# Neighbourhood attention beside a spatial gating unit: logits reduced by column-tiled mask matmuls, tokens strided by four, and two sets of transposes moved from TensorE to DMA

## The chip, the cores and the metric

The kernel runs on one core of one Trainium2 chip. The metric is the device time of one execution in microseconds (us). Times are quoted as medians over several executions, with the lowest and highest in brackets. A profile is one execution taken with the hardware profiler. In it PE is TensorE, PEld its weight loads, DVE is VectorE, ACT is ScalarE, POOL is GpSimd and SP is SyncE, which here only issues DMAs; SPq and ACTq are the DMA queues that SP and ACT issue to. L701 is line 701 of that run's kernel.py. PSUM (`ps`) is where this kernel's matmuls put their results; to copy out of it is called evacuation. The granted clock is the recorded share of TensorE's full clock. An execution counts as slow when it takes over 1.5% more than the fastest of the same kernel; all runs that are compared below are fast unless it is said otherwise.

## The reference

One input `x` of 2048 tokens by 512 goes through two branches, and `x` is added at the end. The inputs are bf16.

```python
def _A_ref(x, wqkv, wo):                    # attention over 8 earlier tokens, 2 apart
    H = 32; Dh = D // H; W, dil = (8, 2)
    qkv = (x @ wqkv).reshape(B, S, 3, H, Dh)...      # cut
    idx = pos[:, None] - off[None, :]; mask = idx >= 0
    logits = einsum('bhsd,bhswd->bhsw', q, kg) * scale
    logits = where(mask, logits, -1000000000.0)
    attn = softmax(logits)
    o = einsum('bhsw,bhswd->bhsd', attn, vg)
    return o.reshape(B, S, D) @ wo

def _B_ref(x, w_in, w_sp, b_sp, w_out):     # Fh = 896
    z = gelu(x @ w_in); z1 = z[..., :Fh]; z2 = layernorm(z[..., Fh:])
    g = einsum('ts,bsf->btf', w_sp, z2) + b_sp       # mixes all 2048 tokens
    return (z1 * g) @ w_out

xn = layernorm(x)
return x + _A_ref(xn, wqkv, wo) + _B_ref(xn, w_in, w_sp, b_sp, w_out)
```

There are 32 heads of 16 elements. Each token looks at 8 keys, so a logit is the sum of 16 products, and there are 2048 x 8 x 32 of them.

## The kernel before

The program hands each instruction to a small static scheduler, which fixes the order on each engine from estimated durations. Two stages follow from the data. Stage 1 makes the normalised `x`, transposes it (`xnT`), and computes Q, K, V, both gate halves (`z1`, `z2`) and the logits. Stage 2 mixes tokens with `w_sp` and multiplies out, since mixing needs all of `z2`. VectorE's attention products with V run beside stage 2.

The logits: VectorE multiplies Q with eight shifted copies of K (one operation of 128 x 4096 for each quarter of the channels). TensorE sums 16 channels to one head by taking a 128-token slice of the products as stationary weights, and an 8-column mask as the moving operand.

```python
for blk in range(4):
    for w in range(8):
        last = t.matmul(ps[:, 3072 + blk * 256 + w * 32 + 8 * c: 3072 + blk * 256 + w * 32 + 8 * c + 8],
                        AC(off["pb"] + 4096 * s_ + 512 * w + 128 * blk, [[1, 128]]), E8,
                        start=True, stop=True)
```

That is a weight load of 128 x 128 and a matmul of 8 columns, 512 times. Normalised `x` and the attention output are transposed by TensorE against an identity and copied out of PSUM by ScalarE; V is copied out by VectorE and written to a DRAM scratch, from which the eight shifted copies are loaded for each block of 128 tokens:

```python
T("dve", lambda v: v.tensor_copy(A("Vn", 512, 512 * sl).rearrange("p (d h) -> p d h", d=16),
                                 bank(k).rearrange("p (h d) -> p d h", d=16)), ...)      # V out of PSUM
...
src = bass.AP(tensor=vscr.tensor, offset=vscr.offset + (16 + 128 * b) * 512,
              ap=[[512, 128], [-1024, 8], [1, 512]])
dma("sp", lambda e: e.dma_start(A("Vs", 4096, 4096 * sv).rearrange("p (w n) -> p w n", w=8), src), ...)
...
for cc in range(4):                                       # attention output, transposed by TensorE
    last = t.matmul(ps[:, 512 * k + 128 * cc: 512 * k + 128 * cc + 128],
                    A("On", 128, 512 * so + 128 * cc), ident, start=True, stop=True)
```

`w_sp` is already transposed by DMA on its way in, four pieces of 2 MB, and the program orders transposing DMAs against all others.

## Time and profile before

The time is 260.27 us (259.58 to 260.78, three runs).

| of the profile before (span 257.5 us) | value |
|---|---|
| TensorE busy | 248.4 us, 96% |
| VectorE busy | 207.6 us, 81% |
| ScalarE busy | 98.1 us, 38% |
| stage 1 on TensorE | from 7.5 to 114.8 us |
| stage 2 on TensorE | to 253.9 us |
| moved by DMA | 39.21 MB |

The prediction shows the main lines. The groups of the kernel before, split by shape, show the logits reduction that the change takes away. The columns are line, engine, operation, destination and source, shapes and count; then busy us and mean ns of one; then idle time of the engine ahead of them.

```profile
L658 PE MATMUL ps<-arena 128*128 128x8 bf16 x512 | 15.1, 166 | 0.8 <-DVE arena L651 0.8
L658 PEld LDWEIGHTS ps<-arena 128*128 128x128 bf16 x512 | 14.9, 96 | 4.3 <-DVE arena L651 1.7
```

The 166 ns is a matmul's length from start to end; what it costs in a pipeline is the distance between starts, 25 ns here, so read costs from the timeline. The weight load of 96 ns is as dense as any other in this kernel. The V copy that moves to ScalarE is 16 x 686 ns on VectorE in the same view.

### The profile page before, as it was taken

The page shows a single profiled execution, that of the slowest core. Times are in us where ns is not written, and L with a number is a line of the kernel's source. Part 1 is how long each engine was busy: PE and PEld are TensorE (multiplying, and loading weights), DVE is VectorE, ACT ScalarE, POOL GpSimd, SP SyncE. Part 2 cuts the span into 40 slices and gives each one's busy share as a digit, 9 for nine tenths or more (in the row PEclk, how much of TensorE's full clock was granted, in tenths as well). Part 3 has the DMA queues.
Part 4 walks back from the last instruction along what each step waited for, and adds up shares of the span by engine and source line. Part 5 has one row for each costly group of instructions (what it writes and reads, how often), then busy time and mean ns, then how long its engine had stood idle before and what let it go on. Part 6 is the DMA issues. An engine that isn't in the chain of part 4 may idle for free.

```text
span 257.5 us, 4109 instructions
## 1 busy us (share of the span) xinstructions
PE 248.4 (96%) x1679; PEld 123.5 (48%) x1706; DVE 207.6 (81%) x297; ACT 98.1 (38%) x185; POOL 31.1 (12%) x57
## 2 busy tenths in 40 slices
PE   6999999999999999999999999999999999999993
PEld 1445546456654645444444444444444444444441
DVE  4859999999979989106999999996589599898651
ACT  2894369688999977773001000010000100001000
POOL 6414563310250040000000000000000000000000
PEclk9999999999999999999999999999999999999999
DMA  7991210100013989979655544789915647330321
GB/s 224 364 347 47 83 45 0 64 20 3 23 61 73 228 197 160 253 159 355 215 186 183 178 168 129 185 202 317 349 48 160 224 124 259 96 114 18 108 83 41
DMA packets 62020, 39.21 MB, mean 152 GB/s; under 512 B 34337, under 2 KB 61361, under 8 KB 62001
## 3 DMA queue, kind: packets, MB, share of 16 engines
q1 hardware_dynamic: 59568, 35.33, 48.6%
q0 software_dynamic: 800, 2.11, 2.3%
q10 hardware_dynamic: 1632, 1.51, 1.8%
q8 instruction: 13, 0.21, 0.3%
q14 instruction: 7, 0.05, 0.1%
HBM read 26.35 MB, written 4.21 MB: 119 GB/s over the span
## 4 chain that ended last, share of the span: by engine, by line
PE 85%; issue 6%; DVE 4%; POOL 1%; POOLq 1%; DMA 1%; ACT 0%; DVEq 0%
PE ps L834 37%; PE ps L890 9%; PE ps L628 8%; PE ps L706 7%; PE ps L753 6%; PE ps L894 5%; PE ps L604 5%; PE ps L658 3%; PE ps L874 1%; PE ps L589 1%; POOLq L375 1%; POOL fpool L739 1%; DVE fpool L572 1%; DMA arena<-in_A_x_dram 1%; DVE arena L651 1%
## 5 line engine op out<-in xcount | busy, mean ns | idle before, releaser
L834 PE MATMUL ps<-arena 128*128 128x512 bf16 x440 | 97.7, 379 | 0.4
L834 PEld LDWEIGHTS ps<-arena 128*128 128x128 bf16 x448 | 43.6, 98 | 51.2
L879 ACT ACTIVATE arena<-ps 128x512 bf16<-128x512 f32 x16 | 9.3, 596 | 124.2 <-PE ps L874 124.2
L858 DVE TENSOR_TENSOR arena<-arena 128x4096 bf16<-128x4096 bf16 x16 | 36.5, 2284 | 0.0
L651 DVE TENSOR_TENSOR arena<-arena 128x4096 bf16<-128x4096 bf16 x16 | 36.0, 2284 | 0.6 <-ACT arena L636 0.6
L628 PE MATMUL ps<-arena 128*128 128x512 bf16 x124 | 28.2, 379 | 0.2
L890 PE MATMUL ps<-arena 128*128 128x512 bf16 x108 | 26.4, 379 | 0.9 <-ACT arena L879 0.7
L706 PE MATMUL ps<-arena 128*128 128x448 bf16 x128 | 27.1, 352 | 0.0
L753 PE MATMUL ps<-arena 128*128 128x512 bf16 x107 | 24.4, 379 | 0.3
L841 DVE TENSOR_TENSOR arena<-ps,arena 128x512 bf16<-128x512 f32 x28 | 19.4, 692 | 4.9 <-PE ps L834 4.0
L901 DVE TENSOR_TENSOR arena<-ps,arena 128x512 bf16<-128x512 f32 x16 | 10.9, 687 | 14.7 <-PE ps L894 13.6
L636 ACT ACTIVATE arena<-ps 128x1024 bf16<-128x1024 f32 x16 | 16.3, 1020 | 10.7 <-PE ps L628 10.5
L860 DVE TENSOR_TENSOR arena<-arena 128x2048 bf16<-128x2048 bf16 x16 | 19.5, 1219 | 0.1
L628 PEld LDWEIGHTS ps<-arena 128*128 128x128 bf16 x128 | 12.4, 98 | 14.5
L758 ACT ACTIVATE arena<-ps 128x512 bf16<-128x512 f32 x28 | 16.2, 597 | 7.1 <-PE ps L753 7.1
L713 ACT ACTIVATE arena<-ps 128x448 bf16<-128x448 f32 x32 | 17.3, 543 | 1.8 <-PE ps L706 1.1
L658 PEld LDWEIGHTS ps<-arena 128*128 128x128 bf16 x512 | 14.9, 96 | 4.3 <-DVE arena L651 1.7
L890 PEld LDWEIGHTS ps<-arena 128*128 128x128 bf16 x112 | 10.6, 98 | 12.4 <-ACT arena L879 0.9
L706 PEld LDWEIGHTS ps<-arena 128*128 128x128 bf16 x128 | 11.7, 97 | 10.1 <-ACT arena L713 1.0
L753 PEld LDWEIGHTS ps<-arena 128*128 128x128 bf16 x112 | 10.6, 97 | 12.3
L894 PE MATMUL ps<-arena 128*128 128x512 bf16 x63 | 16.2, 379 | 0.1
L658 PE MATMUL ps<-arena 128*128 128x8 bf16 x512 | 15.1, 166 | 0.8 <-DVE arena L651 0.8
(59 smaller groups left out, 226.7 us busy)
## 6 DMA issues: line engine op xcount, KB each, us to landing
arena<-vscr SPq DMA_DIRECT2D x16, 1024.0 KB, 5.2
arena<-in_A_x_dram SPq DMA_DIRECT2D x28, 128.0 KB, 3.9
vscr<-arena POOLq DMA_DIRECT2D x16, 128.0 KB, 2.0
out_dram<-arena SPq DMA_DIRECT2D x16, 128.0 KB, 1.7
arena<-in_A_wqkv_dram SPq DMA_DIRECT2D x2, 512.0 KB, 10.0
arena<-in_B_w_in_dram SPq DMA_DIRECT2D x1, 896.0 KB, 11.7
arena<-in_B_w_out_dram SPq DMA_DIRECT2D x1, 896.0 KB, 11.7
arena<-in_A_x_dram ACTq DMA_DIRECT2D x4, 128.0 KB, 4.9
```

Of the source, the lines that this page charges most:

```text
L628: last = t.matmul(bank(k + which), AC(off["wqk"] + 1024 * dc + col0, [[1, 128]]), AC(off["xnT"] + dc * S + 512 * j, [[1, 512]]), start=(dc ...
L651: T("dve", lambda v: v.tensor_tensor(pbv, qb, kb, ALU.mult), reads=rd, writes=[("pb", s_)], est=c_dve(4096, 2.0), name="prod%d_%d" % (j, c ...
L658: last = t.matmul(ps[:, 3072 + blk * 256 + w * 32 + 8 * c: 3072 + blk * 256 + w * 32 + 8 * c + 8], AC(off["pb"] + 4096 * s_ + 512 * w + 12 ...
L706: last = t.matmul(ps[:, 2048 + 512 * hf: 2048 + 512 * hf + 448], AC(off["xnT"] + dc * S + 128 * b, [[1, 128]]), AC(off["w_in"] + 1792 * dc ...
L713: T("act", (lambda c0, hf: lambda a: a.activation(A("z2", 448, FH * b + c0), ps[:, 2048 + 512 * hf: 2048 + 512 * hf + 448], ACTF.Gelu_appr ...
L753: lastm = t.matmul(bank(k), AC(off["w_in"] + 1792 * dc + 128 * fc, [[1, 128]]), AC(off["xnT"] + dc * S + 512 * j, [[1, 512]]), start=(dc = ...
L834: last = t.matmul(bank(k), AC(off["z2"] + FH * sh + 128 * fc, [[1, 128]]), AC(off["wT"] + WSL * r_ + sh * 512, [[1, 512]]), start=(sh == 0 ...
L841: T("dve", lambda v: v.tensor_tensor(tgv, bank(k), A("bbc", 512, 512 * tc), ALU.add), reads=[("ps", k), "bbc"], writes=[("tg", ts_)], est= ...
L858: T("dve", lambda v: v.tensor_tensor(tv, tv, av, ALU.mult), reads=[("attn", j)], writes=[("Vs", sv)], est=c_dve(4096, 2.0), name="pv%d" % ...
L860: T("dve", lambda v: v.tensor_tensor(A("Vs", 2048, 4096 * sv), A("Vs", 2048, 4096 * sv), A("Vs", 2048, 4096 * sv + 2048), ALU.add), writes ...
L890: t.matmul(bank(k), AC(off["z1T"] + fc * S + 128 * tb, [[1, 128]]), AC(off["w_out"] + 512 * fc, [[1, 512]]), start=(fc == 0), stop=False)
L894: last = t.matmul(bank(k), AC(off["OT"] + cc * S + 128 * tb, [[1, 128]]), AC(off["wo"] + 512 * cc, [[1, 512]]), start=False, stop=(cc == 3))
```

## The change

The intent is to shorten TensorE's work. The logits get a layout with heads on partitions: the mask (128 x 32) is stationary and the products stream by, 512 columns at a time, into 32 output partitions; four token groups use four column groups of the array at once (a column group is 32 of its 128 columns, chosen here by the output partitions). Tokens of a block are now every fourth token of 512, so that a 32x32 block transpose on VectorE brings the attention weights back to tokens on partitions. The eight shifted V rows of two blocks of one parity then overlap, so one load of nine rows serves both. The diff, cut to its core:

```diff
+    def tok(b):
+        return (512 * (b // 4) + b % 4, 4) if TMAP else (128 * b, 1)
...
+            if b >= XDMA:                                  # blocks 8 to 15 of x
+                dma("sp", lambda e: e.dma_start_transpose(AC(off["xnT"] + 128 * b, [[S, 4], [1, 128]]),
+                                                          A("xn", 512, 512 * sl)), ...)
+                return
...
-                T("dve", lambda v: v.tensor_copy(A("Vn", 512, 512 * sl)...
+            T("act", lambda a: a.activation(A("Vn", 512, 512 * sl)...
...
+                    for wh in range(2):
+                        for cc in range(4):
+                            sc = (s_ - 3 + cc) % NPB
+                            for g in range(4):
+                                last = t.matmul(
+                                    PC(32 * g * PR + 3072 + 512 * wh, [[1, 512]], 32),
+                                    AC(off["E8"] + 32 * cc, [[1, 32]]),
+                                    AC(off["pb"] + 4096 * sc + 2048 * wh + 128 * g, [[512, 4], [1, 128]]),
+                                    start=(cc == 0), stop=(cc == 3))
...
+                T("dve", lambda v: v.transpose(AC(off["attn"] + 1024 * j, [[32, 8], [256, 4], [1, 32]]),
+                                               AC(off["D"] + d0, [[128, 8], [1, 4], [4, 32]])), ...)
...
+                    src = bass.AP(tensor=vscr.tensor, offset=vscr.offset + (512 * j + 2 + par) * 512,
+                                  ap=[[4 * 512, 128], [1024, 9], [1, 512]])
+                    dma("act", lambda e: e.dma_start(AC(off["Ve"] + 4608 * par, [[512, 9], [1, 512]]), src), ...)
...
-            T("pe", tr, reads=[("On", so), "ident"], ...)            # and its ScalarE copy
+            dma("sp", lambda e: e.dma_start_transpose(AC(off["OT"] + 512 * b, [[128, 4], [1, 128]]),
+                                                      A("On", 512, 512 * so)), ...)
...
-        NWARM = cfg.get("n_warm", 5)
+        NWARM = cfg.get("n_warm", 4)
```

With it come other estimates for the scheduler, other buffers (two places for `w_sp` in place of three), softmax exponentials taken two blocks at a time, x and output traffic on ScalarE's queue, the `wqk` loads ahead of the fifth to eighth block of `x`, and no ordering of transposing DMAs against plain ones.

## The prediction

> **What bounds the kernel now.** I read the busy totals of the page first, then the chain that ended last, then TensorE's timeline, and last the groups and the windows of the other engines.
>
> ```profile
> PE 248.4 (96%) x1679; PEld 123.5 (48%) x1706; DVE 207.6 (81%) x297; ACT 98.1 (38%) x185; POOL 31.1 (12%) x57
> PE 85%; issue 6%; DVE 4%; POOL 1%; POOLq 1%; DMA 1%; ACT 0%; DVEq 0%
> ```
>
> TensorE is busy 96% of 257.5 us and carries 85% of the chain. A busy PE need not be a PE at its peak, so the timeline must tell what one matmul really costs from start to start, and whether there are gaps.
>
> ```profile
> 6.30 0.40 PE L589 MATMUL ps<-arena 128*128 128x128 bf16 x4
> ...
> 37.62 1.68 PE L706 MATMUL ps<-arena 128*128 128x448 bf16 x8
> 39.13 0.61 PE L589 MATMUL ps<-arena 128*128 128x128 bf16 x8
> ...
> 57.33 0.94 PE L658 MATMUL ps<-arena 128*128 128x8 bf16 x32
> 58.13 1.67 PE L706 MATMUL ps<-arena 128*128 128x448 bf16 x8
> ...
> 114.81 24.34 PE L834 MATMUL ps<-arena 128*128 128x512 bf16 x110
> ...
> 146.33 0.39 PE L874 MATMUL ps<-arena 128*128 128x128 bf16 x4
> 146.56 7.07 PE L834 MATMUL ps<-arena 128*128 128x512 bf16 x32
> 153.46 0.39 PE L874 MATMUL ps<-arena 128*128 128x128 bf16 x4
> ...
> 251.54 1.69 PE L890 MATMUL ps<-arena 128*128 128x512 bf16 x7 [0.69 <-ACT arena L879]
> 253.06 1.03 PE L894 MATMUL ps<-arena 128*128 128x512 bf16 x4
> ```
>
> Each row is a start, a length, a line and a count. Start differences give the steps: 32 matmuls of 512 columns from 146.56 to 153.46, so 0.2157 us each; 8 of 448 columns from 37.62 to 39.13, 0.189; a group of four 128-column transposes from 146.33 to 146.56, 0.23; a group of 32 logit reductions (8 columns each) from 57.33 to 58.13, 0.80, so 0.025 each. Hardly a row shows an idle time. The kernel is thus two stretches of dense TensorE work: stage 1 (normalisation, Q, K, V, both gate halves, logits) from 7.5 to 114.8 us, stage 2 (spatial mixing and output) to 253.9, then 3.6 us of last addition and store.
>
> The engine next in line is VectorE:
>
> ```profile
> 20.00:40.00 20.00, 19.87 (x168) 10.81 (x169) 19.18 (x44) 9.97 (x17) 11.60 (x17) 1.00 0.16 55
> 40.00:60.00 20.00, 19.87 (x228) 11.55 (x229) 19.03 (x29) 16.85 (x32) 3.81 (x6) 1.00 0.08 28
> 60.00:80.00 20.00, 19.79 (x212) 11.51 (x213) 18.24 (x26) 19.01 (x40) 4.74 (x5) 1.00 0.08 27
> 80.00:100.00 20.00, 19.02 (x254) 11.17 (x256) 18.89 (x20) 17.19 (x34) 2.99 (x1) 1.00 1.01 190
> 100.00:120.00 20.00, 19.89 (x102) 9.12 (x102) 5.96 (x10) 12.62 (x20) 0.00 (x0) 1.00 0.95 228
> ```
>
> After the bounds come PE, weight loads, DVE, ACT, POOL, then clock and DMA share. In stage 1 VectorE is busy 18 to 19 of every 20 us, and ScalarE up to 19. Both are nearly co-bounds there: a shorter PE stage 1 pays only as far as they are relieved too. The clock is full throughout.
>
> **What the Trainium skill says.** "TensorE: Matmul & The Clock Gate", Back-to-back issue gap, gives N/2.4 + 2.5 ns for a warm matmul and a floor near 25 ns; the steps above (215.7 and 25) agree, so I use them. The same page, Part 3 (Measured speedup vs the span model), gives 2.38 times for three column tiles of 512 columns; "TensorEngine Tiling (Array Packing)", Tiling Modes and Restrictions, says that tiles work in parallel, that a change of tiling mode drains the array, and that column tiling gives up the fast weight load. No tiled matmul is in the trace of before, so nothing here confirms this yet. "SBUF — State Buffer", Door 1, says that strides are free while at least two accesses fall in one 16-byte line; the new weight loads step by 4 bf16, which is exactly two. All old loads are dense (98 ns), so no run shows it. "DMA: Bandwidth & Descriptors", Rules for kernel authors, says that a DMA transpose beside ordinary DMAs needs no ordering; the new kernel drops the ordering that the old one kept, and issues all transposes on SP's queue.
>
> **The change, part by part.**
>
> 1. Logits. Removed: 512 x 0.0245 = 12.5 us of TensorE. Added: 128 matmuls of 512 columns into 32 output partitions, four consecutive ones on four column groups. Perfect overlap makes a round 0.216 us; one block of 32 is 8 rounds, 1.73 us. With the skill's efficiency, 2.38/3 = 0.79, it is 32 x 0.2157 / (4 x 0.79) = 2.18 us, an estimate, in which I let the drains be contained. Four blocks: 8.7. Gain 3.8 us, all on the path.
>
> 2. Attention output transposed by DMA. Removed: 16 x 0.23 = 3.6 us of TensorE in stage 2, plus the 0.69 us wait for the last evacuation shown at 251.54, plus 9.3 us of ScalarE, which has time to spare there. Added: 16 DMA transposes of 128x512. The old 512x2048 one lands in 10.8 us; a sixteenth of its data plus some 2 us of fixed time (a 128 KB store lands in 1.7) is about 2.6 us, an estimate. The schedule puts them a whole mixing block ahead of their readers, the last one seven output blocks (7 x 2.37 us) ahead, so they are hidden.
>
> 3. Half of x transposed by DMA: 8 x 0.23 = 1.8 us off TensorE and 8 x 0.6 = 4.8 off ScalarE in stage 1. These blocks are normalised early, so the latency should be hidden.
>
> 4. V evacuation moves from VectorE (16 x 0.69 = 11 us) to ScalarE. ScalarE pays 16 x 0.6 = 9.5, gets 4.8 back from part 3 and about 5 from two fewer pairs of exp and gelu table loads (1.28 us each). It stays even, VectorE is relieved.
>
> 5. Softmax in the new layout keeps its shapes and adds four 32x32-block transposes of 1024 elements on VectorE, some 1.2 us each at the rate of the 1222 ns one-per-cycle operations. Two of the four tails (4.0 us each) now fall into stage 2.
>
> 6. V loaded once per parity: 8 loads of nine rows instead of 16 of eight, 9.4 MB instead of 16.8. The DMA is off the chain, so this is worth little in itself; it spares buffers. The multiply reads another buffer but keeps contiguous rows of 32, so I leave its 2284 ns.
>
> Sum for TensorE, stage 1: z2 128 x 0.189 = 24.2; Q and K 128 x 0.2157 = 27.6; V 13.8; z1 24.2; eight transposes 1.8; logits 8.7: 100.3 us (before: 105.9 of work in 107.3). To this, 2.4 us of waits. Their place follows from the instruction orders: VectorE now does the rest of the normalisation before the products of the first token block. Adding its steps (16 blocks x 1.35, a gate wave 2.8, four products x 2.2, starting at 3.2 with the early waits for x) makes the products ready near 40 to 42 us; TensorE gets to the first logits block near 41. Its following logits blocks come 1 to 2 us after their products by the same reckoning. One more wait is likely in the first 16 us, where the gate matmuls stand behind transposes. Stage 1: 102.7. Stage 2: 448 + 176 matmuls x 0.2157 = 134.6, waits 0.8: 135.4 (before: 139.1). Span: 7.5 + 102.7 + 135.4 + 3.6 = 249.2. Before, the time is 2.8 us over the span (260.27 against 257.5); so 252.0 us, 3.2% less.
>
> VectorE in all: 207.6 - 11 + 4.9, about 201 us, of which 31 + 71 + 10 + 8 = 120 lie in 135 us of stage 2. It fits, but without much room.
>
> **The rivals.**
>
> A. Column tiles do not overlap. 128 x 0.2157 = 27.6 us replace 12.5: 18.9 worse than reckoned, 271 us. Against it: the skill's measurement and the order of the matmuls, which changes the column group each time. For it: each tile gets new weights at each round, and nothing in the trace speaks to it. Half-way (weight loads not hidden) would be some 3.3 us a block, 256 us.
>
> B. VectorE becomes the bound of stage 1. After each logits block the static order has the maximum wait at once for TensorE, so VectorE loses about 2.2 us four times that it did not lose before, and the products of the next block follow. If that is more than I reckon, TensorE waits at L701 instead of working: 3 to 6 us lost, 255 to 258. For it: 18 to 19 of 20 us busy now. Against it: the 11 us taken off VectorE, and one bank ring of six that lets gate work go ahead.
>
> C. Transposing DMAs queue: those of w_sp hold SP's queue for 7.5 to 8.8 us each, and the small ones stand behind them. Late attention outputs or a late second w_sp block would stop TensorE. By the order this has 10 us of room; if it failed, 2 to 8 us.
>
> D. Strided weight loads take longer than 0.216 us. They hide behind matmuls up to that; at four times 98 ns, 112 of them would cost 0.18 each, 20 us. Two per line speaks against it.
>
> E. Everything overlaps perfectly: 1.8 us a block and no waits, about 248 us.
>
> **Range and chances.** The two percent line is at 255.06. The gain rests on removed TensorE time, which is firm (5.4 us of transposes, 0.7 of tail), and on the tiles (3.8), less new waits (about 2). A and D together get 8%, B or C or half of A beyond the line another 20%. Range 247 to 259.
>
> **What would show it.** Right: L701 blocks of 32 in 1.8 to 2.4 us, starts in fours; TensorE busy sum down by some 9 us; z1 ending near 110, dense L921 and L994 steps of 0.216, and no wait for OT. Wrong: L701 near 7 us a block (A); waits PE <- DVE before L701 of several us and stage 1 ending after 113 (B); waits of L990 or L921 for a DMA (C); L994 steps over 0.22 (D).

## The result, and the profile after

The changed kernel takes 251.31 us (249.38 to 252.22, four runs); the kernel before, run beside it, 260.31 us (259.58 to 260.78, four runs). The ratio is 0.9636, interval 0.959 to 0.9681: faster. A ratio here is the mean time of one kernel's fast runs over that of the other's in the same rounds, so it is not quite the ratio of the medians quoted. The predicted time was 252.0 us, and the predicted span 249.2 us is to the decimal that of the profiled run. The decimal is luck: the four runs span 247.7 to 250.5 us. That the total is hit does not mean that every term was, as the experiments show.

The page of the changed kernel: busy totals, the chain of waits that ended last by engine, and the clock granted in 40 slices.

```profile
PE 240.8 (97%) x1224; PEld 110.3 (44%) x1224; DVE 201.0 (81%) x285; ACT 88.4 (35%) x171; POOL 37.4 (15%) x75
PE 92%; DMA 3%; ACT 3%; issue 1%; SPq 0%; DVE 0%; ACTq 0%
PEclk9799999999999999999999999999999999999999
```

TensorE's busy time is 7.6 us lower and its share of the chain higher: the span fell with TensorE's work, and nothing else took over the end. The second slice of the clock (6.2 to 12.5 us) is new. TensorE's timeline after (start, length, line, count, idle time before it and its releaser):

```profile
5.90 0.40 PE L629 MATMUL ps<-arena 128*128 128x128 bf16 x4 [0.31 <-DVE fpool L612]
7.08 0.40 PE L629 MATMUL ps<-arena 128*128 128x128 bf16 x4 [0.78 <-DVE arena L616]
8.64 4.88 PE L802 MATMUL ps<-arena 128*128 128x448 bf16 x16 [1.17 <-DMA arena<-in_B_w_in_dram]
...
14.74 3.20 PE L802 MATMUL ps<-arena 128*128 128x448 bf16 x16 [0.77 <-ACT arena L633]
17.78 7.07 PE L662 MATMUL ps<-arena 128*128 128x512 bf16 x32
...
44.48 1.91 PE L701 MATMUL ps<-arena 128*32 128x512 bf16 x32
46.33 1.69 PE L802 MATMUL ps<-arena 128*128 128x448 bf16 x8
...
110.98 48.51 PE L921 MATMUL ps<-arena 128*128 128x512 bf16 x224
...
160.19 1.67 PE L994 MATMUL ps<-arena 128*128 128x512 bf16 x7
161.70 1.03 PE L990 MATMUL ps<-arena 128*128 128x512 bf16 x4
```

Differences of starts again: a logits block (L701) takes 46.33 - 44.48 = 1.85 us, 7.4 us for the four, where sixteen groups of 0.80 took 12.8. Stage 1 ends at 110.98 us instead of 114.81. Stage 2 has no idle time; L994, whose weights are now read with a stride, steps by (161.70 - 160.19) / 7 = 0.216 us, as before. The last matmuls end at 245.7 us, so stage 2 takes 134.7 us (139.1 before) and the tail 3.5. The loss is at the start: from 5.90 us to 17.78 TensorE does 6.95 us of work at full rate (16 transposes, 0.92, and 32 gate matmuls, 6.03) in 11.88 us. In the kernel before Q and K begin at 13.87.

Three views of the changed kernel follow: the weight loads of L994 among the groups by shape; VectorE's waits (who waited for whom: sum, times, longest); and the row of the small transposes among the DMA issues (count, median us to landing):

```profile
L994 PEld LDWEIGHTS ps<-arena 128*128 128x128 bf16 x112 | 12.7, 113 | 11.7
```

```profile
DVE fpool L731 <- PE ps L701: 8.3, 3, 3.8
DVE ps L729 <- PE ps L701: 2.8, 1, 2.8
```

```profile
arena<-arena SPq DMA_TRANSPOSE x24, 3.0
```

Strided weight loads take 113 ns instead of 98, and hide. VectorE waits 11.1 us for logits blocks, but TensorE never waits for VectorE after 17.78 us. The new small transposes land in 3.0 us (median); the 16 of the attention output alone in 2.5, the 8 of `x` in 3.7.

### The profile page after: what moved, and what is told of

Its sections match the earlier page's. It is cut to its first block, busy times and chain, and to the rows that moved or that the text cites. A ratio compares the mean times of both kernels' runs of the same rounds, so it can differ in the third digit from the quotient of the medians.

```text
span 249.2 us, 3192 instructions
## 1 busy us (share of the span) xinstructions
PE 240.8 (97%) x1224; PEld 110.3 (44%) x1224; DVE 201.0 (81%) x285; ACT 88.4 (35%) x171; POOL 37.4 (15%) x75
## 2 busy tenths in 40 slices
DMA packets 67775, 34.96 MB, mean 140 GB/s; under 512 B 47264, under 2 KB 67120, under 8 KB 67760
## 4 chain that ended last, share of the span: by engine, by line
PE 92%; DMA 3%; ACT 3%; issue 1%; SPq 0%; DVE 0%; ACTq 0%
PE ps L921 39%; PE ps L802 11%; PE ps L819 10%; PE ps L994 10%; PE ps L662 9%; PE ps L644 6%; PE ps L990 6%; PE ps L701 3%; DMA arena<-in_B_w_in_dram 3%; ACT arena L670 1%; ACT arena L750 1%; ACT arena L633 0%; SPq L551 0%; DVE arena L1001 0%; ACT L750 0%
## 5 line engine op out<-in xcount | busy, mean ns | idle before, releaser
L921 PE MATMUL ps<-arena 128*128 128x512 bf16 x448 | 97.2, 379 | 0.0
L921 PEld LDWEIGHTS ps<-arena 128*128 128x128 bf16 x448 | 43.7, 98 | 52.9 <-ACT arena L824 0.3
L662 PE MATMUL ps<-arena 128*128 128x512 bf16 x128 | 28.3, 379 | 0.0
L994 PE MATMUL ps<-arena 128*128 128x512 bf16 x112 | 26.8, 379 | 0.0
L819 PE MATMUL ps<-arena 128*128 128x512 bf16 x112 | 24.7, 379 | 0.0
L802 PEld LDWEIGHTS ps<-arena 128*128 128x128 bf16 x128 | 12.6, 101 | 15.9 <-issue 1.8
L662 PEld LDWEIGHTS ps<-arena 128*128 128x128 bf16 x128 | 12.5, 98 | 15.1
L824 ACT ACTIVATE arena<-ps 128x512 bf16<-128x512 f32 x28 | 16.0, 600 | 7.4 <-PE ps L819 7.4
L994 PEld LDWEIGHTS ps<-arena 128*128 128x128 bf16 x112 | 12.7, 113 | 11.7
L819 PEld LDWEIGHTS ps<-arena 128*128 128x128 bf16 x112 | 10.8, 98 | 13.5 <-ACT arena L824 0.4
L990 PE MATMUL ps<-arena 128*128 128x512 bf16 x64 | 16.4, 379 | 0.0
L608 DVE BATCH_NORM_STATS2 fpool<-arena 128x6 f32<-128x512 bf16 x16 | 11.0, 685 | 6.1 <-DMA arena<-in_A_x_dram 6.1
L829 ACT ACTIVATE arena<-arena 128x896 bf16<-128x896 bf16 x16 | 15.2, 949 | 0.2
L644 PE MATMUL ps<-arena 128*128 128x512 bf16 x64 | 14.5, 379 | 0.3 <-ACT arena L633 0.3
```

The source lines that it names most:

```text
L644: last = t.matmul(bank(k), AC(off["xnT"] + dc * S + 128 * b, [[1, 128]]), AC(off["wv_raw"] + 512 * dc, [[1, 512]]), start=(dc == 0), stop= ...
L662: last = t.matmul(bank(k + which), AC(off["wqk"] + 1024 * dc + col0, [[1, 128]]), AC(off["xnT"] + dc * S + 512 * j, [[1, 512]]), start=(dc ...
L802: last = t.matmul(ps[:, 512 * k: 512 * k + HF], AC(off["xnT"] + dc * S + 128 * b, [[1, 128]]), AC(off["w_in"] + 1792 * dc + c0, [[1, HF]]) ...
L819: lastm = t.matmul(bank(k), AC(off["w_in"] + 1792 * dc + 128 * fc, [[1, 128]]), AC(off["xnT"] + dc * S + 512 * j, [[1, 512]]), start=(dc = ...
L921: last = t.matmul(bank(k), AC(off["z2"] + FH * sh + 128 * fc, [[1, 128]]), AC(off["wT"] + WSL * r_ + sh * 512, [[1, 512]]), start=(sh == 0 ...
L990: t.matmul(bank(k), AC(off["OT"] + 512 * tb + 128 * cc, [[1, 128]]), AC(off["wo"] + 512 * cc, [[1, 512]]), start=(cc == 0), stop=False)
```

## The experiments

Twelve runs in three sets, each set on one chip beside the kernel before. Medians of before: 262.42 us in the first set (a), 260.73 in the second (b), 260.69 in the third (c).

### a1: the changed kernel again

No edit; the standard for the other runs.

> The changed kernel as it is, again, as the measure for the other runs of this call. Expected 251.3 us within 1 us; the five rounds also tell how wide its spread is (so far 249.4 to 252.2, wider than the 259.6 to 260.8 of the kernel before).

Measured: 251.55 us (250.38 to 252.12), ratio 0.9593 (0.9539 to 0.9648). The result repeats, on a profile with the same slow start (Q and K begin at 19.36 us).

### a2: four matmuls in a row on one column group

```diff
-                        for cc in range(4):
-                            sc = (s_ - 3 + cc) % NPB
-                            for g in range(4):
+                        for g in range(4):
+                            for cc in range(4):
+                                sc = (s_ - 3 + cc) % NPB
```

> Only the order of the 128 logit matmuls is changed: four in a row go to the same column group instead of to four different ones. Theory (the column groups run at the same time): the overlap is lost, a block of 32 takes 32 x 0.216 = 6.9 us instead of 1.85, four blocks cost 20 us more TensorE time, and the kernel takes about 270 us. Rival (a 32-column matmul is simply cheap, whatever the group): blocks stay near 1.85 us and the time at 251.

Measured: 251.65 us (251.13 to 252.28), ratio 0.961. Timeline of this run:

```profile
44.78 1.94 PE L701 MATMUL ps<-arena 128*32 128x512 bf16 x32
46.66 1.69 PE L802 MATMUL ps<-arena 128*128 128x448 bf16 x8
```

A block takes 1.88 us, not 5 or 7. My theory that the order of the column groups makes the overlap has fallen. If matmuls started strictly in program order, each group's four would follow one another and only the last of one group could meet the first of the next: 25 steps of 0.216 us, 5.4 us a block. Counts in stretches of 0.1 us show four of these matmuls at work in the first one already (44.75 to 44.85 us), although the first four in the program go to one group. How this comes about, no run shows. By the time alone, a 32-column matmul could also just be cheap, so b1 follows.

### b1: all matmuls on one column group

Its output is wrong, which doesn't matter for the time. Three quarters of the logits are never written; the outputs differ by 0.68 in relative error.

```diff
-                                    PC(32 * g * PR + 3072 + 512 * wh, [[1, 512]], 32),
+                                    PC(3072 + 512 * wh, [[1, 512]], 32),
```

with the loops as in a2, and a clearing of the bank ahead of the first block.

> Wrong on purpose: all 128 logit matmuls write into one and the same column group (output partitions 0 to 31; the rest of the logits is set to zero once). It answers what the run with four in a row left open: there the time did not change, 251.65, and the counts in short windows showed starts in fours all the same. Theory A (the groups run at the same time, and the engine looks far enough ahead to find work for all four): with one group there is nothing to overlap, 32 x 0.216 = 6.9 us a block, about 20 us more, 271 to 272. Theory B (a 32-column matmul is cheap by itself): still 1.85 us a block and 251 to 253.

Measured: 272.11 us (271.83 to 273.0), ratio 1.0434.

```profile
45.09 7.08 PE L701 MATMUL ps<-arena 128*32 128x512 bf16 x32
```

32 x 0.2157 = 6.9 us: no overlap. So the overlap of column groups is what makes 1.85 us of it, worth 5.05 us a block, 20.2 in all; the time rose by 20.6. This is rival A, made on purpose.

### a3: the old logits reduction in the new kernel

```diff
-    r2=1,
+    r2=0,
```

and a mask laid out for the strided tokens. Tokens stay strided by four, so the products are read as weights with a stride of four elements.

> The logits part alone undone: 512 masked matmuls of 8 columns and the old softmax layout come back, tokens stay strided by 4, so the products are now the stationary operand with a stride of four elements. Theory (the gain of this part is TensorE time): 12.5 us of logit matmuls instead of 7.4, so plus 5.1 us, less nothing: about 256. If a strided weight load costs more than a dense one, these 512 loads, which hide behind only 25 ns of matmul, will show it: at 113 ns instead of 98 perhaps nothing, at four times the pace of dense ones up to 40 us more.

Measured: 260.92 us (259.51 to 261.98), ratio 0.996: the whole gain is gone, 9.4 us more than a1, where 256 was expected. Timeline and weight-load group of this run:

```profile
41.31 1.20 PE L721 MATMUL ps<-arena 128*128 128x8 bf16 x32
42.37 1.02 PE L667 MATMUL ps<-arena 128*128 128x512 bf16 x4
```

```profile
L721 PEld LDWEIGHTS ps<-arena 128*128 128x128 bf16 x512 | 19.6, 117 | 3.3
```

A group of 32 takes 1.06 us where it took 0.80, 33 ns from start to start instead of 25, and a weight load 117 ns instead of 96: these matmuls of 8 columns do not hide it. Sixteen groups cost 17.0 us; less 7.4 this is 9.6, near the 9.4 measured. That it fits so well is partly chance: in the profiled run stage 1 is 8.8 us longer than in a1 (from Q and K on), and stage 2 has a wait of 1.0 us for `wo`. So in this layout the column tiles are worth 9.4 us, more than the 5.4 they save against the dense old reduction.

### b2: the old layout whole

```diff
-    r2=1,
-    vext=1,
-    tmap=1,
+    r2=0,
+    vext=0,
+    tmap=0,
```

> Column tiling, strided tokens and the V load per parity all undone, the DMA transposes and everything else of the change kept; so the old logit matmuls have dense products as weights again. The run with old logits on strided tokens took 260.9, 9.4 more than the changed kernel, where 5.1 were expected; its blocks of 32 took 1.06 us instead of the 0.80 of the kernel before, and 16 x 0.26 = 4.2 is the missing part. Theory (the strided weight load is what made the difference): blocks back at 0.80, 12.8 us of logit matmuls instead of 7.4, so 251.5 + 5.4 = about 257, if the V loads are worth nothing. Rival (the old logits cost more for another reason): about 261 again.

Measured: 287.9 us (285.8 to 289.34), ratio 1.1051, where 257 was expected. The timeline in stage 1 and in stage 2:

```profile
49.15 0.94 PE L716 MATMUL ps<-arena 128*128 128x8 bf16 x32
49.95 1.02 PE L644 MATMUL ps<-arena 128*128 128x512 bf16 x4
...
150.59 1.86 PE L990 MATMUL ps<-arena 128*128 128x512 bf16 x4 [11.37 <-DMA arena<-arena]
...
169.91 26.70 PE L921 MATMUL ps<-arena 128*128 128x512 bf16 x110 [15.00 <-DMA arena<-in_B_w_sp_dram]
```

The first half confirms a3: with dense weights the group is back at 0.80 us. The second half I had not expected: TensorE stands still for 26.4 us, first for a transposed attention output and then for the second piece of `w_sp`, and the mean granted clock falls to 0.95. That is rival C. The switch to V loads per block also changes what the second `w_sp` load waits for, and this run undoes three things at once, so c4 takes the loads alone.

### a4: attention output transposed by TensorE again

```diff
-            dma("sp", lambda e: e.dma_start_transpose(AC(off["OT"] + 512 * b, [[128, 4], [1, 128]]),
-                                                      A("On", 512, 512 * so)), ...)
+            T("pe", otr, reads=[("On", so), "ident"], writes=[("ps", ko)], ...)
+            T("act", lambda a: a.activation(A("OT", 512, 512 * b), bank(ko), ACTF.Copy), ...)
```

The transposes take two PSUM banks, so the output blocks have two in this run instead of four.

> Only the transpose of the attention output goes back to TensorE and ScalarE (64 matmuls of 128 columns and 16 evacuations). Theory: 16 x 0.23 = 3.6 us of TensorE come back in stage 2, plus up to 0.7 us of a wait for the last one: 255 to 255.6. Rival (the DMA transposes themselves held something up, so that the part was worth less): below 253.

Measured: 254.98 us (252.83 to 256.62), ratio 0.9731: 3.4 us over a1. From the first Q and K matmul to the last output matmul it is 231.3 us against 227.9. Part 2 is worth what it was said to be.

### b3: all of x transposed by TensorE again

```diff
-    xdma=8,
+    xdma=16,
```

> Only the transposes of token blocks 8 to 15 go back to TensorE and ScalarE. Theory: 8 x 0.23 = 1.8 us of TensorE come back in stage 1: 253.3. If ScalarE, which gets 8 evacuations more (4.8 us), holds TensorE up besides: up to 255. If this part was hidden anyway: 251.5.

Measured: 255.23 us (253.48 to 256.68), ratio 0.9777. That is 3.7 us over a1 by the medians, 4.8 by the ratios of the two sets. Stage 1 takes 98.1 us from the first Q and K matmul, against 93.2. 1.8 us of this is the transposes. Of the rest, the largest piece is this one:

```profile
95.39 8.81 PE L819 MATMUL ps<-arena 128*128 128x512 bf16 x39 [1.28 <-ACT arena L824]
```

In all the timeline puts 3.4 us of waits down to ScalarE in that stretch, in six rows, and 0.55 to VectorE. Five of the six lack a matmul record (39 for 40, or 15 for 16), so some 1.1 us of the 3.4 is work, and about 2.3 is waiting. In the changed kernel the only such wait after 17.78 us is one of 0.28. So the 4.8 us of ScalarE copies that part 3 removes count too.

### b4 and c3: V copied out by VectorE again

```diff
-            T("act", lambda a: a.activation(A("Vn", 512, 512 * sl).rearrange("p (d h) -> p d h", d=16),
+            T("dve", lambda v: v.tensor_copy(A("Vn", 512, 512 * sl).rearrange("p (d h) -> p d h", d=16),
```

> Only the evacuation of V goes back from ScalarE to VectorE (16 x 0.69 = 11 us). In the changed kernel VectorE waits 11.1 us for the four logits blocks (2.8 + 8.3 in the list of waits). Theory (VectorE has slack in stage 1 now, so this part bought no time by itself): 251 to 253. Rival B of the prediction (VectorE is next to the bound, and this part is what pays for the rest): the products come late, TensorE waits ahead of the logits, 255 to 260.

Measured for b4: 274.49 us (273.71 to 275.36), ratio 1.052.

```profile
130.79 1.91 PE L701 MATMUL ps<-arena 128*32 128x512 bf16 x32
...
156.88 26.68 PE L921 MATMUL ps<-arena 128*128 128x512 bf16 x110 [20.61 <-DMA arena<-in_B_w_sp_dram]
```

Stage 1 is no slower: without the fourth logits block it ends at 109.98 us. But the scheduler, which counts VectorE as late, has put that block into stage 2, and the second `w_sp` load comes after it, by way of the V loads that it is told to wait for. So c3 drops that one dependency.

```diff
-                    ld_wT(1, after=[("Ve", 0), ("Ve", 1)] if VEXT else [("Vs", 1)])
+                    ld_wT(1)
```

> V evacuation on VectorE as in the run that gave 274.5 us, but the second transposing load of w_sp no longer waits for the two V loads (it waits only for its buffer). Theory: the 20.6 us stall of that run was this gate alone, with the fourth logits block being ordered into stage 2; then the stall goes and what remains is what the 11 us of VectorE work cost by themselves: the prediction reckoned VectorE relief as worth 0 to 5 us, so 251.5 to 257 us, no wait of L921 for a DMA over 2 us. Rival: VectorE as such is too late with the softmax and the attention output in stage 2, so TensorE waits for VectorE or for the attention-output transposes by 5 us or more whatever w_sp does: 260 us and over.

Measured for c3: 263.1 us (261.66 to 264.14), ratio 1.008. The wait for `w_sp` is gone, which shows that it was the dependency, and 11.6 us are still lost against a1. The expectation's rival held. VectorE's timeline, TensorE's timeline near the end, and one window of stage 2 (bounds; PE, weight loads, DVE, ACT and POOL busy; clock and DMA share):

```profile
94.67 6.69 DVE L688 TENSOR_TENSOR arena<-arena 128x4096 bf16<-128x4096 bf16 x3
112.91 0.69 DVE L928 TENSOR_TENSOR arena<-ps,arena 128x512 bf16<-128x512 f32 x1 [11.55 <-PE ps L921]
```

```profile
244.50 1.04 PE L990 MATMUL ps<-arena 128*128 128x512 bf16 x4 [3.62 <-DMA arena<-arena]
```

```profile
220.00:240.00 20.00, 19.52 (x91) 9.22 (x90) 19.01 (x23) 0.00 (x0) 0.00 (x0) 1.00 0.47 118
```

VectorE loses 11.55 us in one wait, because the next thing in its order is a mixing result. From 140 to 240 us it is busy 18 to 19 of every 20 us and never makes the loss good, so the last attention outputs are late and TensorE waits 9.4 us for them in five places. Another 2.8 us go to the clock: after the waits of 3.62 and 3.32 us seven matmuls of L994 take 2.92 and 3.18 us instead of 1.67, and the granted clock from 240 to 260 us is 0.83. So it is not shown that the loss is the price of VectorE's 11 us as such, near as the two figures are: it is that work, the place that the order gave it, and the clock together. Whether another order of the same instructions would avoid it was not tried.

### c4: V loaded per token block

```diff
-    vext=1,
+    vext=0,
```

> The changed kernel with V loaded per token block (16 loads of eight rows, 1024 KB each) instead of per parity (8 of nine rows), all else kept. The prediction put this part at about nothing in time (251 to 253 us), since the loads are hidden. Rival, from the run that undid the whole layout (287.9 us): there the sixteen V loads, each behind a buffer, held back the second w_sp transpose and the attention outputs, and TensorE stood still for 26 us in stage 2. If the loads per block are the cause of that, a wait of L921 or L990 for a DMA of 5 us or more shows here too, and the time is 257 to 285 us; if it was the other parts of the layout, none shows. The fall of the traffic of DMA should be undone: 39 MB instead of 35.

Measured: 264.15 us over all four runs. Two of them, 265.16 and 266.12, count as slow by their spread, so there is no ratio; the fast two are 263.14 (the profiled run) and 260.61, still 9 to 12 us above a1. The DMA traffic is 42.30 MB, against 34.96.

```profile
148.18 26.10 PE L921 MATMUL ps<-arena 128*128 128x512 bf16 x112 [6.62 <-DMA arena<-in_B_w_sp_dram]
```

TensorE waits 6.6 us for `w_sp` and 2.7 for VectorE, and pays some 3 us more for a clock that has fallen (112 matmuls in 25.9 us in place of 24.2, seven in 3.2 in place of 1.7). The second `w_sp` load is issued at 133.65 us; in the changed kernel it is issued at 116.36. It is needed near 135 us (110.98 + 112 x 0.2157) and has a median landing time of 10.9 us there. What SP waits for last ahead of it, first in the changed kernel, then in c4 (`prof LABEL --waits --engine SP`: sum, times, longest):

```profile
SPq L264 <- DMA arena<-vscr: 3.9, 1, 3.9
```

```profile
SPq L264 <- DVE arena L969: 2.0, 1, 2.0
```

In c4 this is VectorE and no DMA. The switch also makes this load wait for `("Vs", 1)`, the third VectorE step on the second V block, in place of the two V loads. VectorE starts on that block at 116.23 us, so the bytes are there; but its third step comes at 132.90, behind two softmax tails in VectorE's order. Before this wait, SP's queue is at three `wo` loads until 131.47 us. So the dependency and the order on the queue held the load, as far as the trace shows. What loads per parity are worth by themselves stays open: a run with loads per block and without this dependency was not made, and b2 has it too.

### c1 and c2: the late start

```diff
+        for b in range(4, min(8, NB)):                 # ahead of the wqk loads, as before
+            ld_x(b, "sp" if b % 2 == 0 else "act")
```

The same two lines are taken away behind the `wqk` loads.

> The changed kernel with one thing put back: the loads of the fifth to eighth block of x are issued before those of wqk, as in the kernel before, not after them. In the changed kernel the first Q and K matmul starts at 17.78 us (13.87 before), 0.78 + 1.17 + 0.77 us of that are gaps in TensorE and 1.7 us a slow first gate group (4.72 us for 16 matmuls that take 3.03 later). If the moved loads cause the late start: Q and K begin 1 to 2.5 us earlier and the time is 249 to 250.5 us, some 1 us to 2 us under the changed kernel. If the late start comes from w_in (wait 1.17 us at the first gate group) and the clock alone: no change, 251 to 252 us, and the wait for w_in is longer by as much as the x loads now take from it.

Measured for c1: 251.87 us (250.69 to 252.52), ratio 0.9646: no change, so the moved loads are not what delays the start. Why `w_in` is waited for (0.92 us here) stays open. c2 adds two pairs of warm-up matmuls to c1:

```diff
-        NWARM = cfg.get("n_warm", 4)
+        NWARM = 6
```

> The same load order, and six instead of four pairs of warm-up matmuls, of which some fall by the order between the first transposes and the gate matmuls. If the slow first gate group (16 matmuls in 4.72 us, where they take 3.03 at full clock) is the clock that has fallen back in the gaps before it: that group takes 3.0 to 3.4 us and the time is another 1 us below the run with the load order alone, 248 to 249.5 us, a version that beats both kernels. If more warm-up only takes TensorE time while data is awaited: same as the load order alone within 0.5 us.

Measured for c2: 249.59 us (249.46 to 252.83), ratio 0.9585, with five of six runs between 249.46 and 249.70. One window of one microsecond, first of the changed kernel, then of c1, then of c2 (columns as above):

```profile
10.00:11.00 1.00, 1.00 (x4) 0.44 (x3) 0.00 (x0) 0.64 (x2) 0.00 (x0) 0.50 1.11 356
```

```profile
10.00:11.00 1.00, 1.00 (x4) 0.46 (x3) 0.97 (x5) 0.63 (x2) 0.32 (x1) 1.00 1.10 360
```

```profile
10.00:11.00 1.00, 1.00 (x7) 0.54 (x6) 0.90 (x4) 0.44 (x2) 0.55 (x1) 1.00 1.08 363
```

The third figure from the end is the clock; the count in the first brackets is the matmuls that ran in that window. The changed kernel runs its first gate matmuls at half clock, four in a microsecond; with warm-up matmuls between the first transposes (at 6.14 us in c2) there are seven. Q and K begin at 16.29 us, 1.5 us before the changed kernel and 2.3 before c1, and the span is 2.2 us shorter than in c1. The profile of c1 (and of a1) differs from that of the changed kernel in one point: its four transposes at 7.08 us take 0.61 us, where they take 0.40 in the changed kernel and in c2. So in c1 the matmuls were slow before the gap already, ahead of any added pair, and part of the 2.3 us is how that execution began. The times of all executions speak for the pair: five of the six of c2 are below 250 us, and one of the sixteen of the changed kernel (result and a1) and c1. The kernel before had such a pair in that gap (at 6.54 us); the change went from five pairs to four and lost it. The medians of c1 and c2 are 2.3 us apart, the means 1.6, and the two intervals still overlap slightly, so the size is less sure than the mechanism. More warm-up without the load order was not run. By its median c2 is the fastest version here; by the ratio it cannot be told from a1 (0.9593), which ran beside a slower median of the kernel before.

## Why the prediction was right, point by point

The sum was right because its larger terms were, and because the smaller errors cancelled. Stage 1 ended at 110.98 us for 110.2, stage 2 took 134.7 for 135.4, the tail 3.5 for 3.6.

**Part 1, logits.** The mechanism was right (b1). The term was mis-sized: 1.85 us a block for 2.18, that is 6.9 / 1.85 = 3.7 times for four groups. 7.4 us in all for 8.7, and 12.8 removed for 12.5. The drains that the prediction let be contained can have cost at most 1.85 - 1.73 = 0.12 us a block. The reason given, the order of the groups, was wrong (a2).

**Part 2, attention output.** 3.4 us by a4 against a removed 3.6 plus 0.7. The transposes of this kind land in 2.5 us (median), estimated at 2.6. The queue holds each for 1.2 us (median), which the sum had no term for; TensorE waited for none of them, VectorE once, for 5.1 us.

**Part 3, half of x.** The removed 1.8 us of TensorE is right; b3 gives 3.7 to 4.8. The missing term is ScalarE, which the prediction names ("4.8 off ScalarE") but gives no value.

**Part 4, V by ScalarE.** ScalarE stays even: TensorE waits for it 0.28 us after the start. But it was counted as relief only, worth nothing in the sum. In c3 the same 11 us on VectorE cost 11.6 us in that schedule, part of it through the clock.

**Part 5, softmax.** The block transpose takes 1.245 us for 1.2.

**Part 6, V loads.** That it is "worth little in itself" is neither confirmed nor refuted. c4 is 9 to 12 us slower, but the last wait ahead of its late `w_sp` load is a dependency that came with the switch. The prediction had seen the buffers, not that this load is made to wait for work on V.

**Waits and lead-in.** The logits blocks never waited for their products; the prediction had held part of its 2.4 us of waits ready for the first of them. The start was mis-sized: two waits of 1.17 and 0.78 us, another of 0.77, and 1.7 us of half clock (4.72 us for 16 gate matmuls that take 3.03). The prediction expected "one more wait"; it took the clock as full. This ate the 1.3 us that the logits gave and about 0.8 more. It is also part of why TensorE's busy sum fell by 7.6 us and not by the 9 that the prediction named as a sign.

**From span to time.** In every run whose span is on record, time and span are 1.7 to 1.9 us apart, so the 2.8 us that were added must hold some 1 us of difference between the median and a quicker profiled run. In the run profiled after, time and span are 250.89 and 249.2, 1.7 apart. With it, the same sum gives 250.9.

**The rivals.** A is refuted by b1, which is what it would have looked like. B had the amount right, about 2.2 us four times (11.1 measured), but TensorE had other work in that time. C did not happen in the changed kernel, and happened in b2, b4 and c4, where it cost more than the 2 to 8 us given. D: 113 ns, hidden behind 0.216 us; it bites where the matmul is shorter, in a3. Undone one at a time, the parts give 9.4 + 3.4 + 3.7 + 11.6 + 9 or more, far over the 9 us that the whole gains. So these figures are not the worth of the parts: a removal also breaks the order that was made around it, as b4 and c4 show, and brings costs that the kernel before did not have, such as the strided loads of a3.

## What to carry to other kernels

Cost an instruction by the distance between starts, and cost its removal on every engine that it occupied, not only on the one that bounds. When a change touches work that is "hidden anyway", look for what is told to wait for it: in b4 and c4 the second `w_sp` load was, and TensorE stood still for 20.6 and 6.6 us. When a change alters the first microseconds, look at matmuls per microsecond there: a thin stretch between warm-up and work can bring the clock down again (here 1.1 us of work in 3.4).

## What the Trainium skill lacked or had wrong

- "TensorE: Matmul & The Clock Gate", Part 3, Measured speedup vs the span model, has three column tiles at 2.38 times and none of four. Four column groups of 512 columns ran 3.7 times as fast here (32 matmuls in 1.85 us; 6.9 us on one group).
- The same page, Part 3, The mechanism, says of matmuls that they are in strict order, "no reordering". With four in a row on each group, the block still took 1.88 us (a2), where starts in program order would give 5.4, worked out above.
- "SBUF — State Buffer", Door 1, says that two accesses to a 16-byte line are enough for full bandwidth. Weight loads with a stride of four bf16 took 113 to 117 ns in place of 96 to 98, and 32 matmuls of 8 columns 1.06 us in place of 0.80 (a3 against b2).
- "DMA: Bandwidth & Descriptors", DMA Transpose (X-bar), has no time for a small transpose within SBUF. One of 128 x 512 bf16 held SP's queue for 1.2 to 1.3 us and landed in 3.0 us (median of 24). That no ordering against plain DMAs is needed, as its Rules for kernel authors say, agrees: all runs but b1 were correct.
- "TensorE: Matmul & The Clock Gate", Part 1, What's actually happening, has the clock fall after an idle window of about 3.4 us. Here it fell to half at 8.7 us although the 3.4 us before (5.3 to 8.7) were no idle window: TensorE was busy for 1.1 of them and never idle for over 1.2 at once. With 2.1 us busy in the same stretch (c2) it stayed full. The page's caveat on clock records holds: c1 is recorded at 1.00 while its matmuls run four to the microsecond.
